# Batch 1's k turned by DMA transposes instead of TensorE, with the load queue put in a new order

## The chip, the cores and the metric

The kernel runs on one core of one Trainium2 chip. The metric is the device time of one execution in microseconds (us). Before the change three runs took 226.76, 226.93 and 227.65 us; the median is 226.93 us.

## What is computed

A decayed linear attention ("retention") runs over q, k and v of shape 4 batches x 8 heads x 768 positions x 64, and a mixer follows.

```
for t in range(768):                       # per batch b and head h, gamma from 1 - 2**-5 to 1 - 2**-12
    state = gamma[h] * state + outer(k[b,h,t], v[b,h,t])
    y[b,h,t] = (1/8) * q[b,h,t] @ state
x  = y, heads side by side                 # 4 x 768 x 512
h  = transpose(x) @ U @ V                  # over positions, rank 32
u  = x + transpose(h)
out = u + relu(u @ w_ch1) @ w_ch2          # 512 -> 2048 -> 512
```

All inputs and the output are float32; the kernel multiplies in bfloat16.

## The kernel before

**Attention.** The recurrence is done in six chunks of 128 positions for each batch. The decay is folded into q and v (into q and k in part of batch 0), so that a chunk needs `score` (k times q transposed, masked), `mix` (masked scores times v, plus q times the state, and the state's update) and nothing else. Matmuls contract over partitions, so `score` needs k and q with the head dimension on partitions: each chunk of k and q has to be turned. Batch 0 is handled in units by code of its own (a list of steps, `STEPS`) and turns with matmuls against an identity. Batches 2 and 3 turn k and q with DMA transposes from SBUF to SBUF (`turn_chunk`, L245 to L250). Batch 1, before the change, turns both with matmuls: `turn_k1` (four 128x128 matmuls and one copy out of PSUM for each chunk, copied by ScalarE for even chunks and VectorE for odd ones) and `turn_q1` (the same for q, but from loads that hold four heads and 256 positions, two such pieces for each pair of chunks).

**Mixer.** For each batch it is 24 "up" pieces (`up`, L429, and `up_two`, L442; relu out of PSUM by ScalarE or VectorE) and 24 "down" pieces of four 128x512 matmuls each (`down`, L458). They are nearly all of TensorE's work.

**Order on the engines.** Nothing is scheduled by a planner: every engine runs its instructions in the order in which the program writes them (`manual_schedule`). `weave` walks through one batch's mixer pieces, and before each piece runs the "marks" that are due: a mark at 0.565 comes when 56.5% of the batch's mixer cost is written. During batch b's mixer run the marks of batch b+1's attention: casts (`prep`, `prep_two`), turns, scores of a pair of chunks together (`s0` in the table AT), and mixes (`dm` after that). Chunk numbers below are written (batch, chunk): (2,5) is the last chunk of batch 2.

**SyncE's queue (SP).** All loads of q, k and v, all DMA transposes and the last output store are issued by SP, one after another in program order; an SP instruction that waits holds all behind it. A load of k or v brings one chunk of all heads, 256 KB in pieces of 256 bytes. A load of q for batch 1 (`load_heads`) brings 256 positions of four heads, 256 KB in pieces of 512 bytes. `feed` is the list of loads of batches 1 to 3 in order; `feed_more` issues from it as long as fewer than `n_open` are out and fewer than 20 ring buffers are held. After batch 0, the program opens 2 loads, then 6 after the first quarter of w1 has landed (`feed_behind(511)`), then all 36 of batches 1 and 2 after the second quarter (`feed_behind(1023)`); in both cases the gate is a small copy by GpSimd into the next load's buffer. So before the change the 18 loads of batch 1 and the 18 of batch 2 stand in SP's queue with no transpose among them, and the first six transposes of batch 2, (2,0) to (2,2), stand behind all of these.

**GpSimd's queue (POOL).** It issues the weights' loads (w1 and w2, 1 MB of float32 each, cast to bfloat16 on the way) and the output stores, and it does most casts of q, k and v into bfloat16 (`cast`, L81 and L83), in program order. ScalarE casts k of chunks (1,2) to (1,5) (L77).

**Buffers.** The turned k and turned q each rotate over three buffers (tags kT and qT; `qT1`, two, for batch 1). A bank of PSUM under the tag `mlp` (three of them) serves mixer pieces and TensorE's turns alike.

Of the kernel before, what the change touches and what calls it, by code (L numbers as in the profile page):

```python
# [16 lines left out]
def kernel(  # L17
# [12 lines left out]
    P = 128  # L30
# [97 lines left out]
    def feed_more(t=None):  # L128
        while n_fed[0] < n_open[0] and n_held[0] < RING:
            nm, b, ci = key = feed[n_fed[0]]  # L130
            n_fed[0] += 1
            n_held[0] += 1
            ready[key] = t = ring() if t is None else t
            if (nm, b) == ("q", 1):
                load_heads(t, q, 1, ci % 2, ci // 2)
            else:
                nc.sync.dma_start(
                    out=t.rearrange("p (h d) -> p h d", h=H),
                    in_=src_of[nm][b, :, ts(ci, P), :].rearrange("h p d -> p h d"))
            t = None  # L140
# [64 lines left out]
        feed_more()  # L205

    def prep(nm, b, ci, eng="P"):
        if (nm, b) == ("q", 1):
            return prep_q1(ci)
        src = ready.pop((nm, b, ci)).rearrange("p (h d) -> p h d", h=H)  # L210
        t = rpre.tile([P, H, D], bf16, tag=nm + "d", name=f"{nm}d_{b}_{ci}")
        g = {"k": None, "q": gq, "v": gk}[nm]
        if g is not None:
            g = g[:, ci, :, None].to_broadcast([P, H, D])
        cast(eng, t, src, g)
        pre[nm, b, ci] = t
        n_held[0] -= 1
        feed_more()
# [23 lines left out]
    def open_x(b):  # L242
        xs[b] = xp.tile([P, NCK, DM], bf16, tag="x", name=f"x_{b}")

    def turn_chunk(b, ci):  # L245
        for nm in "kq":
            t = bts[nm, b, ci] = rpre.tile([P, 4, P], bf16, tag=nm + "T",
                                           name=f"{nm}T_{b}_{ci}", bufs=3)
            nc.sync.dma_start(out=t, in_=pre[nm, b, ci].rearrange("p h d -> p (h d)"),
                              transpose=True)  # L250

    def turn_k1(ci):
        t = bts["k", 1, ci] = rpre.tile([P, 4, P], bf16, tag="kT", name=f"kT_1_{ci}",
                                        bufs=3)
        tp = bank("mlp")
        for hp in range(4):
            nc.tensor.matmul(tp[:, ts(hp, P)], pre["k", 1, ci][:, ds(2 * hp, 2)], ident,
                             start=True, stop=True)
        evac("AD"[ci % 2], t.rearrange("p n m -> p (n m)"), tp)

    def turn_q1(ci):
        g, pp = ci % 2, ci // 2
# [297 lines left out]
                                 stop=True)  # L560

    def turned_unit(nm, u, eng):
        t = eb[nm + "T", u] = rpre.tile([P, 2, 2 * P], bf16, tag=nm + "T", bufs=3,
                                        name=f"{nm}t_{u}")
        tp = eb.pop(("tp", nm, u))
        if nm == "k":
            evac(eng, t.rearrange("p n m -> p (n m)"), tp)
        else:
            evac(eng, t.rearrange("p n (t j) -> p n j t", j=2),
                 tp.rearrange("p (n j t) -> p n j t", n=2, j=2))  # L570
# [196 lines left out]
    n_open[0] = 2  # L767
    feed_more()
    load_w1(1024, 512)
    n_open[0] = 6  # L770
    feed_behind(511)
    n_open[0] = 6 * NCK
    load_w1(1536, 512)
    for j in range(4):
        load_w2(j)
    feed_behind(1023)
    for t in nsz:
        nc.gpsimd.memset(t, 0.0)
    for nm in "kqv":
        prep_two(nm, 0)  # L780

    AT = {1: ((0.565, 0.685, 0.80), None, (0.045, 0.09), (0.075, 0.045), None),
          2: (0.255, 0.17, (0.05, 0.095), (0.175, 0.11),
              (0.0, 0.085, 0.17, 0.255, 0.34, 0.425)),
          3: (0.20, 0.20, (0.05, 0.095), (0.19, 0.145),
# [11 lines left out]
    for b in range(1, B):  # L799
        s0, step, dm, dt, at_prep = AT[b]  # L800
        for ci in range(NCK):
            pair_at = b - 1 + (s0[ci // 2] if b == 1 else s0 + step * (ci // 2))
            if b == 1:
                mark(pair_at - dt[0], turn_k1, ci)
                mark(pair_at - dt[1], turn_q1, ci)
            else:
                mark(b - 1 + at_prep[ci], prep_chunk, b, ci)
                mark(pair_at - dt[ci % 2], turn_chunk, b, ci)
            mark(pair_at, score, b, ci)
            mark(pair_at + dm[ci % 2], mix, b, ci)  # L810
            if b > 2:
                mark(b - 2 + 0.25 + 0.1 * ci, open_chunk)
        if b == 1:
            for nm, eng, at in (("k", "A", (0.51, 0.63)), ("q", "P", (0.54, 0.66)),
                                ("v", "P", (0.58, 0.70))):
                for pp in (1, 2):
                    mark(at[pp - 1], prep_two, nm, pp, eng)
            mark(0.905, lr_open, b)
            mark(0.905, lr_proj_turn, b)
            mark(0.94, lr_uT, b)  # L820
            mark(1.11, lr_expand, b, 0, 4)
        else:
            l0, l1, l2, l3 = LR
            mark(b - 1 + l0, mixed, b)
            mark(b - 1 + l1, lr_expand, b, 0, 4)
            mark(b - 1 + l2, lr_turn, b, 0)
            mark(b - 1 + l3, lr_turn, b, 2)
        mark(b + 0.02, lr_expand, b, 4, 2)
        mark(b + 0.08, lr_turn, b, 4)
# [35 lines left out]
```

## Time and profile before

| | |
|---|---|
| time, median of 3 | 226.93 us |
| the profiled execution | 227.32 us, of which the span of the core's instructions is 225.5 us |
| TensorE (PE) busy | 213.9 us, 95% of the span, granted clock 1.00 |
| VectorE, ScalarE, GpSimd busy | 98.6, 82.2, 78.7 us |
| SP's DMA queue (q1) | 83152 packets, 23.86 MB, 46.9% of the 16 DMA engines |
| GpSimd's DMA queue (q0) | 6128 packets, 10.42 MB, 18.5% |
| batch 0's attention | until about 26 us |
| batch 0's mixer, with batch 1's attention in it | 26 to 81 us |
| batch 1's mixer, with batch 2's attention in it | 81 to 130 us |

Busy times of engines overlap. TensorE's matmuls are pipelined, so a line of matmuls is shown a little longer than the pace at which they follow each other. An SP row is the time in which the queue issued one DMA, waiting for room included; the data land later. The DMA row of the page is the mean busy share of the 16 DMA engines.

### The profile page before, as it was taken

How to read it: one execution, taken by the hardware profiler on the slowest of the kernel's cores; microseconds unless marked ns; L12 is line 12 of the kernel's file. 1: busy time of each engine (PE TensorE's matmuls, PEld its weight loads, DVE VectorE, ACT ScalarE, POOL GpSimd, SP SyncE). 2: the span in 40 equal slices, each digit the busy share in tenths (PEclk: the TensorE clock that was granted, in tenths of full speed). 3: DMA queues.
4: the chain of work that ended last, by engine and by line, in shares of the span. 5: the costliest groups of instructions: out<-in, count | busy, mean ns of one | idle time of the engine just before them, and what ended most of it. 6: DMA issues, size and time to landing. Idle time of an engine off the chain costs nothing.

```text
span 225.5 us, 4740 instructions
## 1 busy us (share of the span) xinstructions
PE 213.9 (95%) x1955; PEld 122.6 (54%) x1982; DVE 98.6 (44%) x140; ACT 82.2 (36%) x156; POOL 78.7 (35%) x113
## 2 busy tenths in 40 slices
PE   7978999999899999999999999999999999999991
PEld 2556544775466544487554444587554444764451
DVE  6676646236366165536236144443624242222121
ACT  3766364443643235475230034746030044420000
POOL 5577573026640149580100398630101100001010
PEclk9999999999999999999999999999999999999999
DMA  6999999999999977779998644422114330001211
GB/s 179 328 259 245 185 208 204 196 215 229 300 250 252 284 200 158 175 150 212 167 243 220 171 130 96 93 48 25 47 49 121 114 94 0 0 3 47 93 75 66
DMA packets 89301, 34.58 MB, mean 153 GB/s; under 512 B 71216, under 2 KB 87728, under 8 KB 89280
## 3 DMA queue, kind: packets, MB, share of 16 engines
q1 hardware_dynamic: 83152, 23.86, 46.9%
q0 software_dynamic: 6128, 10.42, 18.5%
q8 instruction: 15, 0.25, 0.4%
q14 instruction: 6, 0.05, 0.1%
HBM read 27.46 MB, written 6.29 MB: 150 GB/s over the span
## 4 chain that ended last, share of the span: by engine, by line
PE 52%; issue 31%; SPq 6%; POOL 4%; DMA 2%; ACT 1%; DVE 0%; POOLq 0%; ACTq 0%
PE mlp L458 18%; PE mlp L429 17%; PE mlp L442 6%; SPq L106 5%; POOL out_dram L408 3%; DMA in<-in_v_dram 2%; PE r L281 2%; PE r L302 1%; PE st L313 1%; PE r L297 1%; POOL vd L83 1%; PE r L344 1%; PE mlp L271 1%; PE mlp L400 1%; POOL qd L83 0%
## 5 line engine op out<-in xcount | busy, mean ns | idle before, releaser
L458 PE MATMUL mlp<-w2b,gT 128*128 128x512 bf16 (+2 forms) x384 | 86.2, 370 | 1.3 <-DVE gT L418 0.3
L420 ACT ACTIVATE gT<-mlp 128x512 bf16<-128x512 f32 x64 | 38.1, 597 | 70.0 <-PE mlp L429 57.1
L458 PEld LDWEIGHTS <-gT 128*128 128x128 bf16 x400 | 36.9, 98 | 39.3 <-issue 0.7
L429 PE MATMUL mlp<-uT,w1b 128*128 128x512 bf16 x243 | 56.1, 379 | 0.3
L408 POOL DMA_DIRECT2D out_dram<-o x24 | 13.3, 553 | 107.5 <-DVE o L465 99.8
L418 DVE TENSOR_SCALAR gT<-mlp 128x512 bf16<-128x512 f32 x32 | 22.1, 690 | 45.4 <-PE mlp L429 23.9
L429 PEld LDWEIGHTS <-w1b 128*128 128x128 bf16 x250 | 23.6, 98 | 27.4 <-issue 0.2
L465 DVE TENSOR_TENSOR o<-mlp,u 128x512 f32<-128x512 f32 (+2 forms) x25 | 16.7, 670 | 44.2 <-PE mlp L458 43.5
L442 PE MATMUL mlp<-uT,w1b 128*128 128x256 bf16 x256 | 29.4, 273 | 0.1
L442 PEld LDWEIGHTS <-w1b 128*128 128x128 bf16 x256 | 24.8, 98 | 3.8
L284 DVE TENSOR_TENSOR a<-r,mask 128x1024 bf16<-128x1024 f32 x18 | 21.2, 1219 | 7.6 <-PE r L281 7.6
L83 POOL TENSOR_TENSOR vd<-in,gk 128x512 bf16<-128x512 f32 x18 | 18.7, 1040 | 10.4 <-DMA in<-in_v_dram 10.2
L70 ACT ACTIVATE x<-r 128x512 bf16<-128x512 f32 x20 | 11.9, 595 | 27.8 <-PE r L302 27.8
L351 DVE TENSOR_TENSOR u<-r,x 128x512 bf16<-128x512 f32 (+1 forms) x16 | 14.6, 951 | 3.6 <-PE r L344 3.6
L83 POOL TENSOR_TENSOR qd<-in,gq 128x512 bf16<-128x512 f32 x12 | 12.5, 1039 | 0.0
L70 ACT ACTIVATE nsz<-st 64x256 bf16<-64x256 f32 x30 | 11.2, 372 | 0.3
L81 POOL CAST kd<-in 128x512 bf16<-128x512 f32 x14 | 8.5, 608 | 6.8 <-issue 6.2
L83 POOL TENSOR_TENSOR qp<-in,gq 128x512 bf16<-128x512 f32 x6 | 6.2, 1045 | 7.6 <-DMA in<-in_q_dram 5.8
L591 DVE TENSOR_TENSOR a<-r,mask 128x1024 bf16<-128x1024 f32 x6 | 7.3, 1222 | 3.0 <-PE r L584 2.9
L302 PE MATMUL r<-vd,a 128*128 128x64 bf16 x144 | 7.1, 193 | 0.0
L281 PE MATMUL r<-qT,kT 64*128 64x128 bf16 x144 | 5.8, 217 | 0.7 <-ACT qT L70 0.5
L302 PEld LDWEIGHTS <-a 128*128 128x128 bf16 x144 | 6.0, 98 | 0.7
(110 smaller groups left out, 151.0 us busy)
## 6 DMA issues: line engine op xcount, KB each, us to landing
in<-in_k_dram SPq DMA_DIRECT2D x24, 256.0 KB, 5.1
in<-in_q_dram SPq DMA_DIRECT2D x24, 256.0 KB, 4.7
in<-in_v_dram SPq DMA_DIRECT2D x24, 256.0 KB, 5.0
out_dram<-o POOLq DMA_DIRECT2D x23, 256.0 KB, 2.7
w1b<-in_moe_w_ch_dram POOLq DMA_DIRECT2D x4, 512.0 KB, 8.4
w2b<-in_moe_w_ch_dram POOLq DMA_DIRECT2D x4, 512.0 KB, 15.9
kT<-kd SPq DMA_TRANSPOSE x12, 2.4
qT<-qd SPq DMA_TRANSPOSE x12, 2.4
```

The lines of the kernel that those rows point to most:

```text
L70: nc.scalar.activation(dst, src, AF.Copy)
L83: e.tensor_tensor(dst, src, scale, op=ALU.mult)
L284: nc.vector.tensor_tensor(a, r.rearrange("p i (n m) -> p i n m", n=4), mask[:, None, None, :].to_broadcast([P, 2, 4, P]), op=ALU.mult)
L302: nc.tensor.matmul(o[:, ts(h, D)], a[:, i, hp], vb[:, h], start=(ci == 0 and h == 0), stop=True, skip_group_check=True)
L351: nc.vector.tensor_tensor(v4(us[b][:, ds(j0, nj), e]), R[g][:, :, :nj * P].rearrange("p c (j e) -> p c j e", j=nj), v4(xs[b][:, ds(j0, nj) ...
L408: eng.dma_start(out=dst, in_=src)
L418: nc.vector.tensor_relu(dst, src)
L420: nc.scalar.activation(dst, src, AF.Relu)
L429: nc.tensor.matmul(g_p[:, :sz], w1b[:, c, ts(m, P)], uTs[b][:, c, ds(lo, sz)], start=(c == 0), stop=(c == NCB - 1))
L442: nc.tensor.matmul(g_p[:, ts(n, S - LO)], w1b[:, c, ts(m + n, P)], uTs[b][:, c, LO:], start=(c == 0), stop=(c == NCB - 1))
L458: nc.tensor.matmul(ch[:, :nn], gT[:, m, ts(j, P)], w2b[:, m, ds(n0, nn)], start=(m == 0), stop=(m == NM - 1))
L465: nc.vector.tensor_tensor(o_sb, ch[:, :nn], us[b][:, j, n], op=ALU.add)
```

## The change

- `turn_k1` goes: the 24 matmuls and six copies out of PSUM for batch 1's k. In their place six DMA transposes are issued by SP, (1,0) to (1,5).
- q of chunks (1,4) and (1,5) is loaded as k and v are (256-byte pieces), cast as batches 2 and 3 cast it, and turned by two DMA transposes; eight matmuls and two copies go. q of chunks (1,0) to (1,3) stays with TensorE.
- `prep_turn` casts a pair of chunks, issues its two transposes on SP and then opens more loads. By it SP's order becomes: k and q of pair 0; transposes of k (1,0), (1,1); v of pair 0; k, q, v of pair 1; transposes of k (1,2), (1,3); k, q, v of pair 2; transposes of k (1,4), (1,5) and of q (1,4), (1,5); the 18 loads of batch 2; then, as before, the transposes of (2,0) to (2,2). The gate `feed_behind(1023)` goes.
- ScalarE casts k of (1,2), (1,3) alone; GpSimd casts k of (1,4), (1,5).
- The tag kT has four buffers instead of three.
- Marks: scores of batch 1's pairs come at 0.555, 0.67, 0.775 instead of 0.565, 0.685, 0.80; the mixes and what follows move with them, and `lr_open`, `lr_proj_turn` and `lr_uT` come 0.02 sooner.

```diff
-            if (nm, b) == ("q", 1):
+            if (nm, b) == ("q", 1) and ci < NCK - 2:
                 load_heads(t, q, 1, ci % 2, ci // 2)
...
     def prep(nm, b, ci, eng="P"):
-        if (nm, b) == ("q", 1):
+        if (nm, b) == ("q", 1) and ci < NCK - 2:
             return prep_q1(ci)
...
+    def turn_dma(nm, b, ci):
+        t = bts[nm, b, ci] = rpre.tile([P, 4, P], bf16, tag=nm + "T",
+                                       name=f"{nm}T_{b}_{ci}", bufs=4 if nm == "k" else 3)
+        nc.sync.dma_start(out=t, in_=pre[nm, b, ci].rearrange("p h d -> p (h d)"),
+                          transpose=True)
+
     def turn_chunk(b, ci):
         for nm in "kq":
-            t = bts[nm, b, ci] = rpre.tile([P, 4, P], bf16, tag=nm + "T",
-                                           name=f"{nm}T_{b}_{ci}", bufs=3)
-            nc.sync.dma_start(out=t, in_=pre[nm, b, ci].rearrange("p h d -> p (h d)"),
-                              transpose=True)
-
-    def turn_k1(ci):
-        t = bts["k", 1, ci] = rpre.tile([P, 4, P], bf16, tag="kT", name=f"kT_1_{ci}",
-                                        bufs=3)
-        tp = bank("mlp")
-        for hp in range(4):
-            nc.tensor.matmul(tp[:, ts(hp, P)], pre["k", 1, ci][:, ds(2 * hp, 2)], ident,
-                             start=True, stop=True)
-        evac("AD"[ci % 2], t.rearrange("p n m -> p (n m)"), tp)
+            turn_dma(nm, b, ci)
+
+    def prep_turn(nm, pp, eng, n_loads):
+        prep_two(nm, pp, eng)
+        for ci in (2 * pp, 2 * pp + 1):
+            turn_dma(nm, 1, ci)
+        n_open[0] = n_loads
+        feed_more()
...
-    n_open[0] = 6
+    n_open[0] = 4
     feed_behind(511)
-    n_open[0] = 6 * NCK
     load_w1(1536, 512)
     for j in range(4):
         load_w2(j)
-    feed_behind(1023)
     for t in nsz:
         nc.gpsimd.memset(t, 0.0)
-    for nm in "kqv":
-        prep_two(nm, 0)
+    prep_turn("k", 0, "P", 12)
+    prep_two("q", 0)
+    prep_two("v", 0)
...
-    AT = {1: ((0.565, 0.685, 0.80), None, (0.045, 0.09), (0.075, 0.045), None),
+    AT = {1: ((0.555, 0.67, 0.775), None, (0.045, 0.09), 0.045, None),
...
             if b == 1:
-                mark(pair_at - dt[0], turn_k1, ci)
-                mark(pair_at - dt[1], turn_q1, ci)
+                if ci < NCK - 2:
+                    mark(pair_at - dt, turn_q1, ci)
...
         if b == 1:
-            for nm, eng, at in (("k", "A", (0.51, 0.63)), ("q", "P", (0.54, 0.66)),
-                                ("v", "P", (0.58, 0.70))):
-                for pp in (1, 2):
-                    mark(at[pp - 1], prep_two, nm, pp, eng)
-            mark(0.905, lr_open, b)
-            mark(0.905, lr_proj_turn, b)
-            mark(0.94, lr_uT, b)
+            mark(0.51, prep_turn, "k", 1, "A", 18)
+            mark(0.54, prep_two, "q", 1)
+            mark(0.58, prep_two, "v", 1)
+            mark(0.64, prep_turn, "k", 2, "P", 18)
+            mark(0.68, prep_turn, "q", 2, "P", 6 * NCK)
+            mark(0.72, prep_two, "v", 2)
+            mark(0.885, lr_open, b)
+            mark(0.885, lr_proj_turn, b)
+            mark(0.92, lr_uT, b)
```

(Batch 0's `turned_unit` is changed only in naming four kT buffers as well.)

More of the change, by code (lines that the diff above doesn't have):

```diff
@@ L562, in turned_unit @@
     def turned_unit(nm, u, eng):
-        t = eb[nm + "T", u] = rpre.tile([P, 2, 2 * P], bf16, tag=nm + "T", bufs=3,
-                                        name=f"{nm}t_{u}")
+        t = eb[nm + "T", u] = rpre.tile([P, 2, 2 * P], bf16, tag=nm + "T",
+                                        bufs=4 if nm == "k" else 3, name=f"{nm}t_{u}")
         tp = eb.pop(("tp", nm, u))
```

## The prediction

> **What bounds the kernel now.** I read the page's slices first, then TensorE's chain where batches 1 and 2 lie, then SP's queue row by row, then the landing of single transposes. The slices, 5.64 us each:
>
> ```profile
> PE   7978999999899999999999999999999999999991
> DMA  6999999999999977779998644422114330001211
> ```
>
> TensorE is full from end to end, and the DMA engines are full too through slice 14 (79 us) and seven to nine tenths full through slice 22 (124 us). So work taken from TensorE is worth its time, and work given to the DMA engines before 110 us is paid for. Next, TensorE by stretch (busy time of PE, PEld, DVE, ACT, POOL, then clock, DMA share, GB/s):
>
> ```profile
> 49.00:56.00 7.00, 6.73 (x60) 3.65 (x61) 4.18 (x6) 2.24 (x5) 4.14 (x4) 1.00 0.95 230
> 56.00:64.00 8.00, 6.78 (x71) 4.05 (x70) 4.46 (x6) 4.62 (x10) 6.17 (x7) 1.00 1.04 271
> 64.00:72.00 8.00, 7.95 (x88) 4.89 (x88) 4.16 (x6) 3.82 (x8) 0.69 (x2) 1.00 1.05 261
> ```
>
> The only hole of size is at 56 to 64: batch 1's turns wait there for each other's copies. The chain of waits gives TensorE's pace and the places of the scores (start, time, what):
>
> ```profile
> 64.09 0.45 PE mlp L257 x8
> 64.54 0.86 PE mlp L458 x4
> ...
> 69.80 0.55 PE r L281 x16
> ...
> 93.62 0.62 PE r L281 x16
> ...
> 102.44 0.55 PE r L281 x16
> ...
> 111.39 0.55 PE r L281 x16
> ```
>
> Eight turning matmuls take 0.45 us, a down piece 0.86, the scores of a pair 0.55. Last, SP's queue, in order of time (start, time of issue, what), and the landing of two transposes, (2,q1) issued at 87.53 and (2,q5) issued at 106.91:
>
> ```profile
> 56.10 2.07 SPq L137 DMA_DIRECT2D in<-in_v_dram  x2
> 58.21 1.88 SPq L137 DMA_DIRECT2D in<-in_k_dram  x1
> ...
> 82.61 0.47 SPq L137 DMA_DIRECT2D in<-in_v_dram  x1
> 83.45 1.32 SPq L249 DMA_TRANSPOSE kT<-kd  x1
> ...
> 90.19 1.22 SPq L249 DMA_TRANSPOSE qT<-qd  x1
> 91.46 0.57 SPq L137 DMA_DIRECT2D in<-in_k_dram  x1
> ...
> 106.91 2.05 SPq L249 DMA_TRANSPOSE qT<-qd  x1
> ```
>
> ```profile
> qT<-qd SPq DMA_TRANSPOSE x1, 2.4
> ...
> qT<-qd SPq DMA_TRANSPOSE x1, 3.7
> ```
>
> The reader is to see that SP never rests between 56 and 109 us, and how little room batch 2's transposes have: (2,q1) is in SBUF at 89.9, and TensorE takes it in the second half of the scores at 93.9, 4.0 us later; (2,q5) is in SBUF at 110.6, and TensorE takes it at 111.67, 1.1 us later.
>
> **What leaves TensorE.** 24 matmuls of k and 8 of q, 32 at 0.45/8: 1.8 us. Between 48.27 (end of the up pieces) and the third pair's scores TensorE has 15 down pieces (12.95), 3 turns of k and 3 of q (2.7), two pairs of scores (1.1) and four mixes (2.45 by the chain), 19.2 us; it starts these scores at 69.8, so it has also stood still for 2.3 us. With k off TensorE these stalls have no cause left (they are copies of kT, casts of k and copies of qT queued on ScalarE behind them). The most that TensorE can win is 1.8 + 2.3 = 4.1 us. The eight copies out of PSUM that go (0.6 us each, half on ScalarE, half on VectorE) lie on engines that are 36% and 44% busy; they count only through those stalls. The marks bring one down piece fewer before the third scores: wanted at 48.27 + 12.1 + 0.9 + 1.1 + 2.45 = 64.8.
>
> **What SP's queue gets, term by term.** A load of 256 KB in a full queue: the 8 issues from 49.83 to 58.16 take 1.04 each, the 18 from 58.21 to 83.08 take 1.38 with output stores between them. A transpose moves half as much, so 0.52 to 0.69 us of the DMA engines where older loads are still queued; where none are, it costs its issue, (91.46 - 83.45)/6 = 1.33 us.
> - Transposes of k (1,0), (1,1): their casts come at 31.4 to 32.6, so SP issues them at about 32 to 35 instead of v's loads at 27.7, when q's loads are still landing under w2 (v's two loads, issued next, take 18.9 us to land before). They take the place of one load: 1.04 to 1.38, I take 1.2, as the queue is full.
> - k (1,2), (1,3): they wait for ScalarE's casts, and the loads of pair 2 wait behind them; ahead is v (1,3), whose data are still queued; one load's place, 1.04, up to two issues, 2.7. I take 1.2: some 4 us of loads lie ahead of SP there (the last load of batch 2 is issued at 82.61 and lands at 86.9).
> - k and q of (1,4), (1,5): four in a row, 2.1 by bytes, 5.3 by issue. They wait for casts that wait for the loads just ahead, and batch 2's loads come only behind them, so the queue runs dry at the end. I take 3.6, nearer the middle.
> - q (1,4), (1,5) in 256-byte pieces: the two issues of 512-byte pieces from 54.69 to 56.05 take 0.69 each against 1.04: +0.6, between 0 and 0.7.
>
> Sum 6.6 us, bounds 4.2 and 10.1. What is queued behind: all 18 loads of batch 2, then its six first transposes.
>
> **Batch 1.** v (1,5) is issued by 58.16 + 1.2 + 1.2 + 0.6 = 61.2 instead of 58.16; the fourth transpose is issued 4.0 later, at 65.2, and lands 2.4 to 3.7 after that, about 68.5. TensorE wants it at 65.1 and stands still 3.4 us. The scores end at 68.8 with 14 pieces done; before they ended at 70.35 with 15. Counting the piece, 0.7 us of the 4.1 are left. v (1,0) lands about 5 us later than before, as a load's bytes now lie ahead of it where v's two casts were 4.9 us apart; its cast was at 44.6, its use at 55.5: covered. The transposes of k (1,2), (1,3) are issued behind v (1,3), at 52.4 to 55.1, and land by 57.5 to 58.8; the second scores are wanted at 58.6 (nine pieces 7.8, two turns 0.9, scores 0.55, two mixes 1.1): nothing, and a stall as long as whatever comes on top. GpSimd takes over two casts of k (0.61 each) and loses a gate of 0.17; it works 0.69 us of the 8 from 64 to 72, so they are hidden, and without that cover they would delay (1,q4) by 1.2.
>
> **Batch 2.** Its first transpose is issued at 83.45 + 6.6 = 90.05, and (2,q1) lands at 96.5. TensorE, 0.7 early, wants it at 93.2; its place before was 93.9. So 2.6 us are lost against before, whatever batch 1 kept. Behind (2,q2) SP has three rounds of three loads and two transposes; from 91.41 to 108.96 they took 17.55. The middle round took 5.08 (97.91 to 102.99); at that pace three take 15.25, because the fourth kT buffer drops the wait for TensorE ahead of (2,k3) and the 2.05 of the last one need not come again. That makes up 2.3. (2,q5) lands at 110.6 + 6.6 - 2.3 = 114.9, against a place of 111.67 before: 3.3 us late, more than 2.6, so this sets the sum. After it, SP's next waits are for VectorE's u, which moves along with TensorE, and TensorE has no idle time that could give it back.
>
> **The sum.** +3.3 us. On the profiled execution (227.32 us, span 225.5) that is 230.6; it stands 0.4 above the median, so 230.2 us.
>
> The row of a transpose and the Trainium skill differ. By Advanced Engine Details and Errata, X-Bar Transpose (TRN2), transposing DMAs are as fast as plain ones; the rows above say so only behind queued loads, and twice the price of the same bytes in a row of transposes. By that rule the four in a row cost 2.1, an estimate from it, and the sum would fall by 1.5 to +1.8. VectorE: DVE Perf Modes, The three transpose paths, speaks against the change: a 128x128 block costs 1309 ns by DMA and 390 by TensorE. Here four blocks go in one DMA of 1.33 us, and a block costs TensorE 0.056 us of pace.
>
> **Rivals.**
> - *Faster: the queue makes it up.* If the transposes ride behind queued loads all through (the low bound, 4.2) and the rounds run at issue speed (3 x 0.62 + 2 x 1.25 = 4.4, making up 4.3), batch 2 stops TensorE by nearly nothing, and the time goes by what batch 1 keeps: 0.7 to 4.1 us, 222.8 to 226.2, say 225. It decides where (2,q1) lands less than 4.0 and (2,q5) less than 1.1 us later than before. Against it: SP and the DMA engines show no rest before 109.
> - *No change.* Lateness at (2,q5) of about 1: 226 to 228.
> - *Much slower.* Each change from loads to transposes may stall the queue: the load just ahead of (2,k5) landed 4.5 us after its issue's end (by the trace's completion of that DMA), the three after (2,q3) 2.6 to 3.3. Three new such places at 1.2 to 1.9 us on top of the sum: +6.9 to 9.0, 233.8 to 235.9.
> - *The loss sits in batch 1*: the stall at the third scores is 6 rather than 3.4. Batch 2 then wants its transposes later, and the end stays at about +3.3: it changes the picture, not the time.
>
> **How the numbers follow.** Forecast 0.64 (including the last rival), with its own range 227.8 to 232.5: from lateness 0.9 to 5.5, the bounds of the sum less what the rounds can make up. Faster 0.20, no change 0.08, much slower 0.08. The range 225.0 to 233.0 leaves out half of the faster case and the much slower one. About 0.5%, 1.1 us, is what a measurement of this kernel can tell from no change; faster by more 0.19, within 0.09, slower 0.72.
>
> **What would show it.** Right: no turn of k on TensorE before 70 us and no hole at 56 to 64; a hole of some 3 us before the third scores at 68; the first transpose of batch 2 issued near 90; holes before the scores of batch 2, the first about 3 us. Wrong: that transpose issued before 87.5, or batch 2's scores starting before 92.

## The result, and the profile after

The changed kernel takes 235.31 us (median of 4 runs, 234.16 to 235.76) against 227.29 us for the kernel before beside it. The ratio is 1.0346, 95% interval 1.0299 to 1.0392: the change makes the kernel 8 us slower. The forecast was 230.2 us with a range of 225.0 to 233.0, so its sign was right and its size was too small by 5 us. The profiled execution, the shortest of the four, took 234.16 us, of which the span is 232.4 (before: 227.32 and 225.5); the readings below are of that one.

The page's slices of the changed kernel, 5.81 us each, counted from 0 in the text:

```profile
PE   7988899997966999999979999999999999999992
PEclk9999999999995899999999999999999999999998
DMA  6999999999899999578999654541012530001212
```

Two things are new. TensorE has a dip at slices 11 to 12 (64 to 75 us), with a clock of 0.5 and 0.8 at slices 12 and 13, and one at slice 20 (116 us). The DMA engines, which had their looser stretch at 79 to 101 us before, have it at slices 16 to 18 (93 to 110 us): everything on them lies later. By stretch (busy time of PE, PEld, DVE, ACT, POOL, then granted clock, DMA share, GB/s):

```profile
56.00:64.00 8.00, 6.44 (x63) 3.62 (x64) 3.36 (x4) 3.25 (x8) 5.27 (x7) 1.00 0.98 232
64.00:72.00 8.00, 4.57 (x53) 2.72 (x50) 1.12 (x2) 2.47 (x6) 5.55 (x7) 0.91 1.10 185
72.00:80.00 8.00, 7.50 (x54) 4.04 (x55) 3.10 (x3) 1.28 (x4) 0.54 (x1) 0.66 1.19 273
112.00:120.00 8.00, 6.76 (x59) 3.49 (x57) 3.39 (x4) 1.59 (x4) 0.58 (x1) 1.00 1.02 195
```

The hole at 56 to 64 has not gone (6.44 busy, 6.78 before): GpSimd's casts of q of (1,2) and (1,3) end there 1.09 and 0.61 us too late for TensorE, as their loads land at 55.8 and 56.5 instead of 51.9 and 52.7. The stretch from 64 to 72 has lost 3.4 us, and moves 185 GB/s where it moved 261. The chain of waits names what the scores stood for (start, time, what):

```profile
70.02 2.34 DMA qT<-qd
...
72.50 0.61 PE r L282 x8
73.11 3.52 PE mlp L459 x8
...
99.43 0.55 PE r L282 x16
...
115.10 3.47 DMA qT<-qd
...
118.70 0.40 PE r L282 x8
119.11 1.83 PE mlp L459 x8
```

The third scores of batch 1 end on the last transpose, that of (1,5). Eight 128x512 matmuls behind them take 3.52 us, at half clock; at 119.11 eight of them take 1.83. Batch 2's first scores start at 99.43 (93.62 before) and wait for nothing: TensorE itself is 5.8 us late there. Its last scores wait 1.24 us for (2,5), and their second half runs at 118.70 (111.67 before). SP's queue (start, time of issue, what; x2 is two issues in a row):

```profile
64.76 2.91 SPq L248 DMA_TRANSPOSE kT<-kd  x2
67.76 3.48 SPq L248 DMA_TRANSPOSE qT<-qd  x2
71.29 0.57 SPq L137 DMA_DIRECT2D in<-in_k_dram  x1
...
90.97 2.11 SPq L248 DMA_TRANSPOSE kT<-kd  x1
...
100.11 0.57 SPq L137 DMA_DIRECT2D in<-in_k_dram  x1
...
115.10 1.57 SPq L248 DMA_TRANSPOSE qT<-qd  x1
```

The first load of batch 2 is issued at 71.29 instead of 58.21, batch 2's first transpose at 90.97 instead of 83.45, and the last, (2,q5), lands at 118.57 instead of 110.6: 7.95 us later, of which come off the 1.05 us that it had to spare before (from its landing at 110.6 to its use at 111.67; called its room below). The span grew by 6.9.

### The profile page after: what moved, and what is told of

Same layout as the page of the kernel before. It is cut to its first block, busy times and chain, and to the rows that moved or that the text cites. A ratio compares the mean times of both kernels' runs of the same rounds, so it can differ in the third digit from the quotient of the medians.

```text
span 232.4 us, 4692 instructions
## 1 busy us (share of the span) xinstructions
PE 217.4 (94%) x1950; PEld 121.9 (52%) x1950; DVE 96.3 (41%) x136; ACT 78.9 (34%) x150; POOL 79.9 (34%) x114
## 4 chain that ended last, share of the span: by engine, by line
PE 58%; SPq 20%; DMA 9%; issue 5%; POOL 5%; ACT 0%; DVE 0%; POOLq 0%
PE mlp L459 27%; PE mlp L430 18%; SPq L137 11%; PE mlp L443 6%; SPq L106 5%; DMA in<-in_v_dram 5%; SPq L248 3%; DMA qT<-qd 3%; DMA in<-in_q_dram 2%; PE r L282 1%; PE r L303 1%; POOL w2b L234 1%; PE r L298 1%; PE st L314 1%; POOL kd L81 1%
## 5 line engine op out<-in xcount | busy, mean ns | idle before, releaser
L459 PE MATMUL mlp<-w2b,gT 128*128 128x512 bf16 (+2 forms) x400 | 89.3, 376 | 0.0
L430 PE MATMUL mlp<-uT,w1b 128*128 128x512 bf16 x250 | 56.8, 379 | 0.0
L83 POOL TENSOR_TENSOR vd<-in,gk 128x512 bf16<-128x512 f32 x18 | 18.6, 1041 | 13.9 <-DMA in<-in_v_dram 13.9
L83 POOL TENSOR_TENSOR qd<-in,gq 128x512 bf16<-128x512 f32 x14 | 14.5, 1042 | 0.0
L81 POOL CAST kd<-in 128x512 bf16<-128x512 f32 x16 | 9.8, 617 | 9.5 <-issue 6.2
L282 PE MATMUL r<-qT,kT 64*128 64x128 bf16 x144 | 6.4, 227 | 5.2 <-DMA qT<-qd 5.2
L282 PEld LDWEIGHTS <-kT 64*128 64x128 bf16 x144 | 4.4, 97 | 8.9 <-issue 4.6
```

Of the source, the lines that this page charges most:

```text
L83: e.tensor_tensor(dst, src, scale, op=ALU.mult)
L430: nc.tensor.matmul(g_p[:, :sz], w1b[:, c, ts(m, P)], uTs[b][:, c, ds(lo, sz)], start=(c == 0), stop=(c == NCB - 1))
L459: nc.tensor.matmul(ch[:, :nn], gT[:, m, ts(j, P)], w2b[:, m, ds(n0, nn)], start=(m == 0), stop=(m == NM - 1))
```

## The experiments

Ratios are against the kernel before on the same chip. Where none is given, there was no interval.

### Which part makes the loss: the queue or TensorE

The first kernel has TensorE's gain without the eight transposes: it leaves out the turns, so its scores in batch 1 are not the reference's, and only its time counts.

```diff
     def turn_dma(nm, b, ci):
+        if b == 1:
+            bts[nm, b, ci] = pre[nm, b, ci].rearrange("p h d -> p (h d)").rearrange(
+                "p (n m) -> p n m", n=4)
+            return
```

> The changed kernel without any turn of batch 1's k and of q (1,4), (1,5): neither TensorE nor a DMA turns them, the scores of batch 1 take the cast data as they are (left out: these turns). Load order, casts and marks stay. If the eight transposes are the loss (queue theory), all of the 4.1 us that TensorE can win appears: 222.5 to 224.5 us, no hole before the third scores, batch 2's first transpose issued at 83 to 85. If the new order of the loads or q in 256-byte pieces is the loss, it stays at 229 us or more.

Measured: 226.85 us, ratio 0.9982 [0.9943, 1.0021]; the loss is gone, but the gain that was expected did not come. This was the most useful miss. TensorE reached batch 2's scores at 90.09, 3.5 us early, and then stood (start, time, what, and in brackets the idle time before it):

```profile
107.93 0.40 PE L286 MATMUL r<-qT,kT 64*128 64x128 bf16 x8
111.36 0.40 PE L286 MATMUL r<-qT,kT 64*128 64x128 bf16 x8 [3.03 <-DMA qT<-qd]
```

(2,q5) landed at 111.2, no earlier than before the change. The prediction had read from the page that TensorE is full and so bounds the kernel; in fact SP's queue was as long as TensorE's, with 1.05 us between them at (2,5), and as long as the queue stands so, nothing that spares TensorE time before 111 us can bring more than that. The second kernel is the other half: the eight transposes go to tiles that nobody reads, and TensorE turns as before.

```diff
     def turn_dma(nm, b, ci):
-        t = bts[nm, b, ci] = rpre.tile([P, 4, P], bf16, tag=nm + "T", ...)
+        tag = nm + ("T" if b > 1 else "X")
+        t = rpre.tile([P, 4, P], bf16, tag=tag, ...)
...
+                mark(pair_at - dt[0], turn_pe, "k", ci)
```

> The eight transposes stand in SyncE's queue where the change puts them, but into spare tiles that nothing reads; TensorE turns k and q of batch 1 as before the change and the scores have their old marks. Queue theory: no hole before the third scores and no half clock in batch 1, but batch 2's transposes land some 7 us later than before and its last scores wait about 5 to 6: 231 to 234 us. If TensorE's stall in batch 1 and the half clock behind it are the whole loss, there is no stall here: 226.5 to 228.5.

Measured: 235.5 us, 1.0332 [1.026, 1.0405]; batch 2's first transpose at 91.43, (2,q5) landed at 117.98, the span 7.3 us longer. The queue alone makes the whole loss, and more than the 231 to 234 expected. But TensorE, held up in batch 1 no more than before the change, paid at another place than the one expected:

```profile
95.11 0.40 PE L294 MATMUL r<-qT,kT 64*128 64x128 bf16 x8 [0.72 <-DMA qT<-qd]
99.04 0.61 PE L294 MATMUL r<-qT,kT 64*128 64x128 bf16 x8 [3.53 <-DMA qT<-qd]
...
118.86 0.62 PE L294 MATMUL r<-qT,kT 64*128 64x128 bf16 x16
```

It waited 4.25 us at batch 2's first scores, the clock was at half from 97.14 to 103.97 us, and the last scores ran without a wait, 0.9 us after (2,q5) had landed. The wait of 5 to 6 us expected there did not come.

The third kernel asks whether the half clock at 70.6 to 77.4 us costs anything: 14 matmuls of zeros fill TensorE's hole.

```diff
+    def warm(n):
+        for _ in range(n):
+            nc.tensor.matmul(R[0][:, 0], zeros[:, :P], zeros, start=True, stop=True)
...
+            if (b, ci) == (1, 4):
+                mark(pair_at, warm, 14)
```

> The changed kernel with 14 matmuls of zeros (3.0 us) put in front of the third scores, where TensorE stands still for 3.4 us. If the stop sets the half clock off and the half clock sets the time, the clock stays full and 2 to 2.5 us come back: 232.5 to 233.5. If batch 2's queue sets the time, the clock stays full but at most 1.2 us come back, as (2,q5) still lands at about 118: 234 to 235.3.

Measured: 235.88 us, 1.0374 [1.0329, 1.0419], in the profiled execution at a clock of 1.00 throughout. The slow clock was gone and nothing came back: TensorE reached batch 2's scores 2.4 us sooner (96.98), and then waited for the queue three times, 1.56, 0.36 and, at (2,5), 1.47 us instead of 1.24:

```profile
118.83 0.40 PE L286 MATMUL r<-qT,kT 64*128 64x128 bf16 x8 [1.47 <-DMA qT<-qd]
```

(2,q5) landed at 118.69. Up to (2,5) it is the queue that sets the time of the changed kernel.

### Fewer transposes

Only k of the first two pairs is turned by DMA; the last pair's k and q stay with TensorE.

```diff
+                if ci >= NCK - 2:
+                    mark(pair_at - 0.075, turn_k1, ci)
...
-            mark(0.64, prep_turn, "k", 2, "P", 18)
-            mark(0.68, prep_turn, "q", 2, "P", 6 * NCK)
+            mark(0.51, open_all)
+            mark(0.64, prep_two, "k", 2)
+            mark(0.68, prep_two, "q", 2)
```

> Four transposes instead of eight: k of pairs 0 and 1 by DMA as in the change, k and q of pair 2 by TensorE from 512-byte pieces as before the change, marks of pair 2 and of what follows as before. Queue theory: the four in a row behind v (1,5) are over half of the delay: batch 2's first transpose is issued 2.5 to 3.5 us later than before the change instead of 7.5, no hole before the third scores: 225 to 229 us. If the first four, beside the weights' loads, are the loss: 231 or more.

Measured: 232.48 us (four executions: 229.21, 232.27, 232.68 and 235.53). The queue was better than expected (batch 2's first transpose at 85.28, (2,q5) landed at 113.57), the time much worse. The stretch that tells why, in the execution of 232.27 us, first the wait, then the window:

```profile
113.71 0.61 PE L295 MATMUL r<-qT,kT 64*128 64x128 bf16 x8 [3.47 <-DMA qT<-qd]
```

```profile
112.00:120.00 8.00, 6.29 (x37) 3.39 (x38) 1.23 (x1) 1.24 (x3) 0.00 (x0) 0.57 1.08 239
```

The scores are 2.0 us later than before (113.71 against 111.67), but the span is 5.0 longer: the wait of 3.47 us brought a clock of 0.57 in this window, half speed from 112.18 to 119.01 us. TensorE worked in 5.3 us of that stretch, which by this halving is a loss of about 2.7 us, and behind (2,5) it waits for no queue that would cover it. The execution of 229.21 us had a mean clock of 0.999 and was 3.1 us shorter, which agrees. In the changed kernel the same slow stretch lay ahead of (2,5) and was free.

### Can the queue be emptied by moving batch 3's loads

Three rounds of loads for batch 3 stand among batch 2's transposes. Four kernels move all 18 loads of batch 3 behind (2,q5): the changed one, the one without turns, the one with four transposes, and the kernel before.

```diff
-                mark(b - 2 + 0.25 + 0.1 * ci, open_chunk)
+                mark(b - 2 + 0.50 + 0.05 * ci, open_chunk)
```

> The changed kernel with one thing moved: batch 3's 18 loads stand behind batch 2's last transposes in SyncE's queue instead of between them, three by three. Queue theory: (2,q5) then lands near 109, before TensorE wants it (117.2 in the changed kernel), so the 1.2 us of its last wait go and what batch 1 lost (5.8 us: the wait for the third scores and the half clock behind it) stays: 233 to 234.3 us. If the rest of the queue, not these loads, holds (2,q5): 235 or more.

> As the run without turns (batch 1's k and q (1,4), (1,5) are not turned at all, which is left out), and batch 3's loads moved behind (2,q5). That run reached batch 2's first scores 3.5 us early and then stood still 3.0 us for (2,q5), which landed at 111.2. Queue theory: with the loads out of the way (2,q5) lands near 100, the wait goes, and the gain of TensorE's work appears at last: 222.8 to 224.3. If something else eats it behind 111 us: 226 to 227.5.

> The run with four transposes (k of pairs 0 and 1 by DMA, pair 2 by TensorE), and batch 3's loads moved behind (2,q5). That run reached batch 2's first scores 1.5 us early, without a wait, and lost 3.5 us and a half clock at (2,q5). Queue theory: these go: 225 to 226.2, faster than before the change. If the early queue sets the time: 228 or more.

> The kernel before with that one move of batch 3's loads alone. Before the change TensorE had 1.05 us of room at (2,q5) and no wait there, so both theories say no change: 226.3 to 227.5. It is the base for the two runs above.

Measured, in this order: 240.39 us (1.0589 [1.0537, 1.0642]); 231.61 us (two executions of 229.2 and 229.4, two of 233.8 and 234.3); 234.96 us (1.0345 [1.0287, 1.0402]); 234.0 us (1.0295 [1.0244, 1.0345]). The queue theory's times were missed in all four. In the kernel without turns the wait at (2,5) did go, and batch 2's last scores came 4.7 us earlier than before the change, but the kernel before shows what came instead:

```profile
135.58 1.87 PE L429 MATMUL mlp<-uT,w1b 128*128 128x512 bf16 x4 [5.14 <-DMA uT<-u]
```

The transposes of batch 2's u stand behind the 18 loads. They are issued at 128.55 instead of 122.81, and TensorE waits 5 us for them (5.17 in the changed kernel, 5.00 without turns). The kernel with four transposes is told by its times alone, as its trace is of one execution that took 368.21 us.

So the loads were given two stretches: chunks 0 to 2 behind (2,q5), one chunk behind the second pair of u's transposes, two behind q's transpose of (3,1).

```diff
-                mark(b - 2 + 0.25 + 0.1 * ci, open_chunk)
+                mark(b - 2 + (0.50, 0.55, 0.60, 0.905, 1.06, 1.07)[ci], open_chunk)
```

> Four transposes only (k of the first two pairs; the last pair's k and q turned by TensorE), and batch 3's loads placed in two stretches: chunks 0 to 2 after the last transposes of batch 2, chunk 3 behind the second pair of u's transposes, chunks 4 and 5 behind q's transpose of (3,1). Theory 'SP's queue has room if its loads are put into its gaps': no stall of over 1 us at (2,5) (3.47 us with the loads among the transposes) nor ahead of u's transposes (5.1 us with all 18 behind), and 224.5 to 226.5 us. Rival 'the queue is full from 26 to 131 us, so that a moved load only moves the stall': one stall of 2 to 5 us at one of these places or at batch 3's first scores, and 229 to 233 us.

> Leaves out every turn of batch 1's k and of q of chunks (1,4) and (1,5), so that its scores read tiles that nothing turned; batch 3's loads in two stretches as in the four-transpose kernel with the split. It has all of TensorE's gain (3.5 us at batch 2's first scores) and none of the change's transposes. Theory 'room': no stall at (2,5), none ahead of u's transposes, 222.5 to 224.5 us. Rival 'full queue': 226 to 232 us, with a stall of over 2 us at one of them.

> The kernel before with nothing but batch 3's loads in two stretches, as in the four-transpose kernel with the split. Theory 'room': the 5.14 us ahead of u's transposes, which the kernel before had with all 18 loads behind (2,5), are gone, and as (2,5) had 1.05 us to spare anyway, nothing else moves: 226 to 228 us. Rival 'full queue': a stall of 2 us or more between 106 and 140 us, 229 to 233 us.

Measured: four transposes 228.6 us, 1.0072 [1.0038, 1.0106]; no turns 226.99 us, 0.9976 [0.9939, 1.0013]; the kernel before with this split 228.71 us, 1.0065 [1.0043, 1.0088]. The large stalls are gone, so the queue does have room; the times still missed. Without turns TensorE came to (2,5) 2.2 us early and gave it back in batch 3, 0.98 us at u's last pair and 1.19 at (3,3), where the six last loads lie just ahead. With four transposes batch 1 lost 2 us against the first kernel of that kind (waits of 1.64 and 0.61 us for casts of q, then half clock from 57.3 to 60.7 us). The kernel before waited 0.84 us at (3,3).

One more chunk in the first stretch, so that one only lies ahead of batch 3's transposes:

```diff
+                mark(b - 2 + (0.50, 0.55, 0.60, 0.65, 0.905, 1.06)[ci], open_chunk)
```

> Leaves out every turn of batch 1's k and of q of chunks (1,4) and (1,5), so that its scores read tiles that nothing turned; batch 3's loads in two stretches, one chunk earlier than in the first split (chunks 0 to 3 after the last transposes of batch 2, chunk 4 behind the second pair of u's transposes, chunk 5 behind q's transpose of (3,1)). The first split lost 0.98 and 1.19 us at the transposes of batch 3, which stood behind its six last loads. Theory 'TensorE's gain can be kept where the loads fit the gaps': no stall over 0.5 us after 90 us, 223.5 to 225.5 us. Rival 'the queue has no such gap': stalls of 1 us or more in sum at (2,5), at u's transposes or at (3,3), and 226 to 229 us.

Measured: 224.69 us, 0.9876 [0.9837, 0.9916], as the theory of room had it. Behind 62 us TensorE's longest wait is 0.16 us. This is what the change was able to bring if its transposes had cost nothing: 2.7 us, and only with batch 3's loads put elsewhere too. What the second split alone does to the kernel before was not run, so how much of the 2.7 us is its own is open.

### What a transpose costs the queue: its place or its turning

In the changed kernel the eight transposes become plain copies of the same tiles, at the same places of the queue.

```diff
     def turn_dma(nm, b, ci):
...
+        if b == 1:
+            nc.sync.dma_start(out=t.rearrange("p n m -> p (n m)"),
+                              in_=pre[nm, b, ci].rearrange("p h d -> p (h d)"))
+            return
```

> The changed kernel with its eight DMA transposes of batch 1 replaced by plain copies of the same tiles from SBUF to SBUF in the same place of the queue (1 KB pieces): k of batch 1 and q of (1,4) and (1,5) are copied and not turned, so the scores of batch 1 are not the reference's. Theory 'it is the place in the queue and the bytes, with their waits for casts, not the turning': the first transpose of batch 2 is issued at 89.5 to 91.5 (90.97 with transposes), 233.5 to 236 us. Rival 'the turning is what costs': a copy is issued in 0.6 us or less, batch 2's first transpose at 84.5 to 87.5, and 228 to 231.5 us.

Measured: 230.68 us, 1.0163 [1.0112, 1.0215]. Batch 2's first transpose is issued 2.75 us later than before, against 7.52 with transposes:

```profile
86.20 1.61 SPq L252 DMA_TRANSPOSE kT<-kd  x1
```

In one trace each, the other kernels with all eight transposes have it at 91.01 to 91.92, those without any turn at 81.37 to 84.53, so the difference is clear of their scatter. Place, bytes and waits for casts cost 2.75 us; transposes instead of copies cost the other 4.77. One thing besides the turning differs: the copies went in packets of 1 KB (46 ns each), the transposes in packets of 256 bytes (18 ns), which by these times comes to 1.7 us of all engines for the eight, an estimate; copies in 256-byte pieces were not run. By pairs, a copy's issue took 0.6 to 1.0 us, a transpose's 1.3 to 1.7 (12.2 us for the eight against 6.2). That is not all of it, as the DMA engines' own rows show. First the changed kernel, 34 to 42 us, 0.2 us for each place:

```profile
DMA  9999999999999999999999940600069999999999
GB/s 223 205 215 215 220 208 220 212 205 210 220 200 218 200 211 196 187 196 205 157 137 91 27 9 13 18 12 8 12 106 202 188 198 195 197 198 239 186 188 188
```

And the kernel with copies, the same stretch:

```profile
DMA  9999999999999999999999999999999999999999
GB/s 220 205 215 205 212 220 202 215 228 251 241 320 220 213 223 230 251 236 246 202 229 189 211 201 202 200 204 188 195 197 200 192 192 195 200 205 187 188 205 202
```

From 38.4 to 39.8 us the engines all but stand, the weights' loads with them: 8 to 27 GB/s move, where some 200 moved before and after. It begins when the last load ahead of the first pair of transposes lands, at 38.35. The same comes at the last four (changed kernel, 66 to 72 us, 0.15 us for each place):

```profile
DMA  9999999999999999940000008999995000089930
GB/s 266 336 329 319 336 304 263 326 299 309 300 280 343 174 125 91 26 2 2 7 9 10 10 9 196 294 260 200 282 285 93 0 0 0 15 203 292 278 85 1
```

The stop from 68.4 to 69.6 lies where the first of the four comes up behind (1,5)'s v; the two gaps after 70.5 are a queue that has run dry. Summed over the single packets of the trace, those that took over 0.4 us make up 2.56 us of all 16 engines between 36 and 40 us and 2.26 us between 68 and 72, 4.8 us together, and nothing in the kernel with copies. That this is close to the 4.77 us is not shown to be more than chance. The kernel with the queue alone has 2.69 and 2.42 at the same two places. The queue's total says the same (packets, MB, share of 16 engines), changed kernel and copies:

```profile
q1 hardware_dynamic: 88528, 24.91, 49.5%
```

```profile
q1 hardware_dynamic: 85328, 24.91, 46.2%
```

Of spans of 232.4 and 229.5 us that is 115.0 and 106.0 us for the same bytes. Why the engines stop is not shown. The kernel before has such a stop too, at 108.2 to 109.4 us (9 to 33 GB/s) ahead of (2,k5), and no stop ahead of its first six.

The Trainium skill has it that transposing DMAs are as fast as plain ones (Advanced Engine Details and Errata, X-Bar Transpose (TRN2)). A single packet agrees: one of 256 bytes takes 18 ns (the median) in the kernel before where only loads and stores move, from 70 to 74 us, and where only transposes do, from 87.2 to 91.4. The queue does not: 7.52 us for eight transposes against 2.75 for eight copies of the same bytes in larger packets.

### Transposes from ScalarE's queue

If the loss were SP's time, another issuer would save it. ScalarE issues the eight, first with all loads written ahead of them, then with the loads written between them, each also with the loads of batch 3 in the last split.

```diff
-        nc.sync.dma_start(out=t, in_=pre[nm, b, ci].rearrange("p h d -> p (h d)"),
-                          transpose=True)
+        eng = nc.scalar if b == 1 else nc.sync
+        eng.dma_start(out=t, in_=pre[nm, b, ci].rearrange("p h d -> p (h d)"),
+                      transpose=True)
...
+            mark(0.45, turn_two, "k", 0)
+            mark(0.56, turn_two, "k", 1)
+            mark(0.695, turn_two, "k", 2)
+            mark(0.72, turn_two, "q", 2)
```

> The changed kernel with the eight transposes of batch 1 issued by ScalarE, each pair some 5 us ahead of its scores, and SP's loads and gates in the order of the kernel before. Theory 'the loss is SP's: issuing and standing still with loads behind it': batch 2's first transpose is issued at 83 to 85.5 (83.45 before, 90.97 with the change), (2,q5) lands at 110 to 112.5, and 225.5 to 228.5 us. Rival 'it is the DMA engines' time, whoever issues': batch 2's first transpose at 87.5 to 91, (2,q5) after 115, and 231 to 235.5 us.

> The kernel with ScalarE's transposes, with batch 3's loads in two stretches as in the second kernel without turns. Theory 'the loss is SP's': (2,q5) early by over 2 us, no stall over 1 us after 90 us, 223.5 to 226.5 us. Rival 'DMA engines' time': batch 2's first transpose at 87.5 to 91, 229 to 234 us.

> ScalarE issues the eight transposes of batch 1 as in the first kernel of that kind, but the loads are opened between them (12 before the first pair, 18 behind it, 24 behind the second, 36 behind the last), so that the DMA eight places before each transpose has landed by then. Theory 'the loss is SP's: issuing and standing still with loads behind it': no stop of ScalarE over 3 us, batch 2's first transpose issued at 83 to 86 (83.45 before, 90.97 with the change), 225.5 to 228.5 us. Rival 'it is the DMA engines' time, whoever issues': batch 2's first transpose at 87.5 to 91, and 231 to 235.5 us.

> The same with batch 3's loads in two stretches, four chunks after the last transposes of batch 2, one behind the second pair of u's transposes, one behind q's transpose of (3,1), which without any turn gave 224.69 us. Theory 'the loss is SP's': no stall over 1 us after 90 us, 224.5 to 226.5 us, faster than both kernels. Rival 'DMA engines' time': 228 to 234 us.

Measured: 246.98 us (1.0863 [1.0817, 1.0909]), 247.06 (1.0883 [1.0852, 1.0914]), 247.96 (1.0912 [1.0859, 1.0965]) and 246.84 us (1.0827 [1.0782, 1.0872]). None of them answers the question. In the first of them, TensorE and ScalarE's queue:

```profile
61.63 1.01 PE L270 MATMUL mlp<-ident,qp 128*128 128x128 bf16 x8 [13.91 <-ACT gT L419]
```

```profile
58.33 2.61 ACTq L249 DMA_TRANSPOSE kT<-kd  x2
```

ScalarE stood from 45.8 to 58.33 before its first transpose, whose input was cast by 31.1, and TensorE then lacked relu outputs for 13.9 us. In all four kernels the issue follows the landing of (1,5)'s load of q by 0.07 to 0.08 us (58.25 and 58.33, 59.38 and 59.46, 58.74 and 58.82, 59.12 and 59.19). The traces' semaphores (the counters by which a DMA tells that it has landed) explain it: the DMAs of SP and ScalarE take the same eight in turn. In all four kernels ScalarE's first transpose has the one that this load of q had last, number 105, and the row before the transpose is ScalarE's wait for number 105, which ends at 58.29 in the first of them. Writing the loads between the transposes did not change whose semaphore it got. What these runs do show is that the engines' stops are not SP's: in the third kernel, with ScalarE issuing, the DMA engines move 8 to 31 GB/s from 69.6 to 71.0 us.

### The part that is worth having

Only k of (1,2) and (1,3) is turned by DMA, with the last split of batch 3's loads (the edit is against the changed kernel).

```diff
-                if ci < NCK - 2:
-                    mark(pair_at - dt, turn_q1, ci)
+                if ci // 2 != 1:
+                    mark(pair_at - 0.075, turn_k1, ci)
+                mark(pair_at - dt, turn_q1, ci)
...
-                mark(b - 2 + 0.25 + 0.1 * ci, open_chunk)
+                mark(b - 2 + (0.50, 0.55, 0.60, 0.65, 0.905, 1.06)[ci], open_chunk)
...
             mark(0.51, prep_turn, "k", 1, "A", 18)
...
+            mark(0.51, open_all)
```

> Only k of (1,2) and (1,3) is turned by DMA transposes, in the place they have in the changed kernel; all else of batch 1 is turned by TensorE, and batch 3's loads are in two stretches (four chunks after (2,q5), one behind the second pair of u's transposes, one behind q's transpose of (3,1)). Theory 'the loss came from the places where all DMA engines stop, and the second pair has none': TensorE gains 8 matmuls (0.45 us) and some of the stall before the second scores (0.5 us), batch 2's first transpose is issued by 85 us, no stall over 1 us after 90 us: 225 to 227 us. Rival 'each change from loads to transposes costs its 1.2 us or more and ends in batch 1': the second or third scores 1 us or more late, 227.5 to 230 us.

Measured: 226.36 us against 227.37, 0.9944 [0.9904, 0.9983], inside the 225 to 227 expected. It is 0.6% faster than the kernel before. How much of that is the split and how much the pair was not measured apart. The reason given was not right: the second pair has a stop as well, at 54.8 to 56.4 us in this kernel's trace (of an execution of 229.14 us, the longest of the twelve).

## Why the prediction was wrong

**Sign, and the path at the end: right.** The loss comes through SP's queue: without the transposes it is gone, and with them alone it is whole. In the changed kernel it ends at (2,5), and there the time is the lateness of (2,q5) less its room, as the prediction put it: 7.95 less 1.05 is the 6.9 us of the span. Where TensorE loses the time on its way there was not right: the prediction had it 0.7 us early behind batch 1 and held up at batch 2's first scores by 2.6 us; measured, it came there 5.8 us late and was not held up. With the transposes alone nearly all was lost at batch 2's first scores.

**How much there is to explain.** Of the 5.1 us between forecast and median, 3.6 are in the profiled execution (230.6 put for it, 234.16 measured), and these are followed below. The other three executions were 1.1 to 1.6 us longer and left no trace.

**The queue's sum: nearly right, by terms that were not.** 6.6 us was put for batch 2's first transpose, and 7.5 measured. But the first pair of transposes, put at 1.2, made k of (1,2) land 2.9 us later (53.1 for 50.2). The second, 1.2, added 2.2 (k of (1,4) lands at 61.6, before 56.5). With the last four, batch 2's first load was issued 13.1 us later (71.29). The 18 loads behind made up 5.6 of it: they took 19.7 us from the first issue to the first transpose, where they had taken 25.2. That the sum still came near the measured one is luck. The prediction priced each transpose as a share of a full queue and looked for no stop of the engines. By the rows of before there was one, the load just ahead of (2,k5), which landed 4.5 us after its issue, and it set that aside for a rival of 0.08.

**The failing step: what the rounds make up.** The prediction let batch 2's three rounds of three loads and two transposes run at the pace of the middle one before, 5.08 us each, and so make up 2.3 us. They took 6.0, 5.1 and 5.5 us (before: 6.5, 5.1 and 6.0) and made up 0.9. The fourth kT buffer did take away the wait ahead of (2,k3), 0.8 us before and 0.1 after, but the first transpose of each round was issued no faster than before: in 2.74, 1.66 and 1.80 us, where it had been 2.52, 1.45 and 1.48 (why it is dear behind loads is not shown). The six transposes ahead of the rounds, put as unchanged at 8.0 us, took 9.1, as the first of them was issued in 2.11 instead of 1.32 us and the next came 0.5 us behind it. With 0.9 too little in the sum, these 1.1 and 1.4 us take (2,q5) from the 114.9 that was put to within 0.3 of the measured 118.57. The *much slower* rival, new stalls at changes from loads to transposes, had the size (233.8 to 235.9 us) and part of the cause: two of its three new places in batch 1 had long stops. Those are within the 7.5 us, though, and not on top of the sum; in batch 2 the changes were as dear as before, where the prediction had let them get cheaper.

**The range.** It was also narrower than its own terms. The upper bound of the sum, 10.1, less the 2.3 that the rounds were to make up and the room of 1.1, is a lateness of 6.7 us and not 5.5; the working does not say where 5.5 comes from. The measured 6.9 lies near that bound.

**TensorE's 4.1 us: unreachable.** The prediction weighed them against the queue term by term; without any turn TensorE did win 3.5 us and the time did not move, since (2,q5) landed no sooner. The rival *faster* could not have reached its 225 us while (2,q5) landed where it did: the room of 1.05 us, which the prediction had read, limits the gain to about that, and the kernel without any transposes took 226.85.

**Batch 1.** The stall at the third scores was put at 3.4 us, ending at 68, and measured at 3.35 and 0.57 us, ending at 71.31 and 72.50. The hole at 56 to 64 was to go and stayed, for q's casts instead of k's turns: the second scores' "nothing" failed, because q of (1,2) and (1,3) landed 3.9 us late. The prediction had followed k's and v's loads there, not q's. Batch 2's scores had no hole before them, since TensorE itself was 5.8 us late; that is the rival *the loss sits in batch 1*, of which the prediction said rightly that it changes the picture and not the time.

**The clock.** The prediction had none in it. The eight matmuls at 73.11 lost 1.7 us by it, and the kernel with matmuls in the hole shows that the slow stretch cost nothing at the end here. In the kernels with four transposes and with the queue alone it did cost: there it lay behind the last wait.

## What to carry to other kernels

A full engine is not yet the bound: before work is taken from it, read at each hand-over how long before its use the other side's result was ready. Here 1.05 us of room at one transfer capped a gain of 3.5 us, and the 2.7 us that came at last needed a second edit as well. A transfer put into a full queue is priced by an experiment that puts it there with nobody reading it; here the first two pairs were priced at 1.2 us each from rows elsewhere in the trace and made the loads behind them 2.9 and 2.2 us later, and no price had a stop of the engines in it. And where a late transfer hits depends on who is late beside it: the same queue cost TensorE its time at (2,1) in one kernel and at (2,5) in another.

## What the runs showed of the hardware

- DMA transposes within SBUF that come up behind loads can all but stop the 16 DMA engines for 1.2 to 1.6 us (2 to 33 GB/s moved), other queues' transfers included, whether SP or ScalarE issued them; plain copies of the same tiles did not, in larger packets. What decides whether a stop comes is not shown.
- TensorE's clock went to 0.5 after or during waits of 2.92 (the copies), 3.35 (the changed kernel), 3.47 (four transposes) and 3.53 us (the queue alone), and after two of 1.64 and 0.61 us close together, and stayed at 1.00 after one of 3.03 us (no turns). In these five kernels the stretch at half clock lasted 3.4 or 6.8 us. With four transposes it began 1.95 us into the wait. The Trainium skill (TensorE: Matmul & The Clock Gate, Part 1: The HAM clock gate) speaks of free-running windows of about 3.4 us, an idle one of which halves the clock. That the length of a wait alone does not decide, and the length of the slow stretches, agree with such windows; a drop 1.95 us into a wait does not agree with a window that has to be idle all through.
- A DMA's issue can wait for the landing of a DMA that has nothing to do with it, on another queue, because both have the same semaphore: TensorE stood 13.4 to 14.0 us behind it in the four kernels with ScalarE's queue.
